# A new hand-written order for the first stage of windowed attention with two gated MLPs on one Trainium2 core

## The chip, the cores and the metric

The kernel runs on one core of a Trainium2 chip. The metric is the device time of one execution in microseconds (us); lower is better. The engines of the core are TensorE (PE, its weight loads shown apart as PEld), VectorE (DVE), ScalarE (ACT), GpSimd (POOL) and SyncE (SP), which issues all DMAs of this kernel.

## What is computed

```python
def _attn_ref(q, k, v):                      # 4 x 8 heads x 576 positions x 64
    scores = scale * np.matmul(q, k.transpose(0, 1, 3, 2))
    rel = pos[:, None] - pos[None, :]
    mask = (rel >= 0) & (rel < 64)           # each row sees itself and the 63 before it
    attn = softmax of scores under the mask
    return np.matmul(attn, v)

x = attention, as 2304 tokens x 512
x = (sigmoid(x @ w_gate) * (x @ w_val)) @ w_out        # d_ff 1536
out = ((x @ w_a) * (x @ w_b)) @ w_out2                 # d_ff 1536
```

The weights come as 64-bit floats and are decoded on the chip to pairs of a high and a low part (`wa`, `wb`, `wo` for gate, value and output). Every product is made of three: high by high, high by low, low by high.

## The kernel before

**Attention.** The 2304 tokens are 18 tiles of 128. One tile is `attention(t, dst, c0)` (line 123), a generator: each `yield` ends a step. Its steps: load `k` and `q` (three buffers for both together, tag `kq`); four transposes of `k` into a PSUM bank (`kps`), a copy of it to SBUF (`kt`, line 148, by `moved`, on VectorE or ScalarE as the table `OTHERS` says) and a copy of the 64 columns before (line 153, ScalarE or GpSimd); the same for `q` (`qps`, `qt`); 16 pairs of score products into two banks (`sps`, line 170); on VectorE four masked minima for each of the two banks (line 183, with `mask_n`, or with an edge mask from `edge_mask(s)`, line 90, for the tiles 0, 4, 9 and 13 in which a sequence starts); four exponentials for each half with their sums on ScalarE (line 189); a copy of the tile's values shifted by 64 rows (`vb`, two DMAs that wait for the load of `v`, lines 198 and 202); the denominators on VectorE (lines 207, 208) and the division on GpSimd (line 210, `pr`); transposes of `pr` (`tps`, line 218) and their copies (`pt`, line 221, `moved` again); the products with the values (`xps`, line 228); and the split of the result into `xh` (ScalarE, line 235) and `xl` (VectorE, line 237), which the first MLP reads.

**First MLP.** Turn n of `FIRST` (line 566) takes a block of 256 tokens or two and some of the 12 slices of d_ff: 12 products for the gate (`gps`) and 12 for the value (`vps`), line 428, then the hidden values on ScalarE and VectorE (`hr`, `hh`, `hl`), then their products with `wo` (`accm`, line 528). Turn 1 is block 1 with slice 0, turn 3 is block 2 with slice 0.

**What sets the order.** Up to its last element the first stage is written out by hand: the string `RAMP` (line 570) names in each letter the stream whose next step is emitted. `a` to `l` are the attention steps of tiles 0 to 11, `V` loads values, `L` loads a weight (line 354 or 352), `D` and `W` are decode steps (lines 374 to 406: ScalarE `low`, `ex`; VectorE `wi`; GpSimd `wi`, line 387; then `ex`, the high part, the low part, line 401), `K` saves a decoded weight to DRAM, `P` is a group of MLP products, `T` what follows them. `in_order()` then ties each engine to this order. So every engine has one queue, and whatever waits at its head holds all that stands behind it. SP is such a queue too: a `vb` copy that waits for its `v` holds the loads behind it.

**Banks.** The pool `ps_at` has three PSUM banks. From tile 4 on all of `kps`, `qps`, `sps`, `tps` and `xps` take them in turn, so each needs the reader of the bank three places earlier to be done. Tiles 0 to 3 transpose `k` and `q` through the two banks of `ps_acc`, and tiles 0 and 1 put their scores in the three of `ps_gv`.

The rest of the program, past the first stage, is put in order by the scheduler.

Of the kernel before, what the change touches and what calls it, by code (L numbers as in the profile page):

```python
# [10 lines left out]
F32 = mybir.dt.float32  # L11
# [4 lines left out]
ALU = mybir.AluOpType  # L16
# [5 lines left out]
def tile_window_attention_gated_mlps(ctx, tc, q, k, v, w1g, w1v, w1o, w2a, w2b, w2o, out):  # L22
    nc = tc.nc
# [14 lines left out]
    WIN = 64  # L38
    KW = P + WIN
    QSCALE = -1.0 / float(D) ** 0.5  # L40
    MASKED = 1.0e30
# [21 lines left out]
    for _ in range(7):  # L63
# [2 lines left out]


    OTHERS = {
        "k": (5, 6, 7),
        "q": (2, 4, 5, 6, 7, 8),  # L70
        "sum": (0, 7, 10),
        "p": (0, 1, 5, 8, 10),
        "norm": (10,),
        "before": (6, 7, 10, 12, 13, 14, 15, 16, 17),
    }
    mask_n = qp.tile([P, P], F32, name="mask_n")
    nc.gpsimd.memset(mask_n, 0.0)
    for e in range(2):
        rows = slice(e * WIN, (e + 1) * WIN)
        nc.gpsimd.affine_select(  # L80
            out=mask_n[rows], in_=mask_n[rows], pattern=[[1, P]], compare_op=ALU.is_ge,
# [3 lines left out]
            out=mask_n[rows], in_=mask_n[rows], pattern=[[-1, P]], compare_op=ALU.is_ge,  # L85
# [3 lines left out]

    def edge_mask(s):  # L90
        m = qp.tile([P, P], F32, tag="mask_s", name="mask_s")
        nc.vector.tensor_copy(m, mask_n)
        nc.vector.memset(m[s * WIN:(s + 1) * WIN, 0:WIN], MASKED)
        return m

    lo, hi = slice(0, D), slice(D, P)
    before, own, last = slice(0, WIN), slice(WIN, KW), slice(P, KW)
# [25 lines left out]
    def attention(t, dst, c0):  # L123
# [41 lines left out]
        for j in range(NP):  # L165
            for turn in range(2):
                for e, dims in enumerate((lo, hi)):
                    s = (e + turn) % 2
# [7 lines left out]
        for e in range(2):  # L176
            if e == 0:
                stat = small.tile([P, 3, 2, NP], F32, tag="stat", name=f"stat{t}")
                ssum, nmax, den = (stat[:, i] for i in range(3))
                mask = edge_mask(starts[0]) if starts else mask_n  # L180
            pr.append(work.tile([P, NP, P], F32, tag="pr", bufs=4, name=f"pr{t}_{e}"))
            for j in range(NP):
                nc.vector.tensor_tensor_reduce(  # L183
                    out=pr[e][:, j, :], in0=sps[e][:, j, :], in1=mask,
                    scale=1.0, scalar=LARGEST, op0=ALU.add, op1=ALU.min, accum_out=nmax[:, e, j:j + 1],
                )
            yield
            for j in range(NP):
                nc.scalar.activation(
                    out=pr[e][:, j, :], in_=pr[e][:, j, :], func=AF.Exp, bias=nmax[:, e, j:j + 1], scale=-1.0,  # L190
                    accum_out=None if t in OTHERS["sum"] else ssum[:, e, j:j + 1],
                )
            yield True
# [10 lines left out]
        for e in range(2):  # L204
            if t in OTHERS["sum"]:
                nc.vector.tensor_reduce(out=ssum[:, e], in_=pr[e], op=ALU.add, axis=AX.X)
            nc.vector.tensor_scalar(out=den[:, e], in0=ssum[:, e], scalar1=1.0e-9, scalar2=None, op0=ALU.add)
            nc.vector.reciprocal(out=den[:, e], in_=den[:, e])
            yield
            (nc.vector if t in OTHERS["norm"] else nc.gpsimd).tensor_tensor(  # L210
                out=pr[e], in0=pr[e], in1=den[:, e].unsqueeze(2).to_broadcast([P, NP, P]), op=ALU.mult
            )
            yield True
# [50 lines left out]
    def attention_units(blk):  # L264
        if blk in BACK:
            if not back:
                back.update(((i, j), quarter(i, j, "xq").bitcast(F32)) for i in range(2) for j in range(2))
        elif (0, (blk,)) not in x:
            new_x(0, group_of[blk])
        for i in range(TB):  # L270
            if blk in BACK:
                half, c0 = divmod((blk - BACK[0]) * N + i * P, W)
                yield blk, attention(blk * TB + i, [back[g, half] for g in range(2)], c0)
            else:
                yield blk, attention(blk * TB + i, x[0, (blk,)], i * P)
# [115 lines left out]
    def decode_pair(F, i, nm):  # L391
        wf, wi = wordy.pop((F, nm))
        nc.vector.scalar_tensor_tensor(  # L393
            out=wf, in0=wf, scalar=SMALLEST, in1=wi.bitcast(F32), op0=ALU.is_ge, op1=ALU.mult
        )
        yield
        pair = wts.tile([P, 2, DM], F32R, tag=f"w{nm}", name=f"w{nm}")
        wh, wl = pair[:, 0, :], pair[:, 1, :]
        nc.scalar.activation(out=wh, in_=wf, func=AF.Copy)
        yield  # L400
        nc.vector.tensor_tensor(out=wl, in0=wf, in1=wh.bitcast(F32), op=ALU.subtract)
        parts.setdefault(F, {})[nm] = (wh, wl)
        pairs[F, nm] = pair
        yield
        if nm != "o":
            nc.sync.dma_start(out=kept[F, "f"][:, i], in_=wf)
            yield
# [3 lines left out]
    def decode(F):  # L411
        for i, nm in enumerate("abo"):
            if nm not in parts.get(F, {}):
                whole(decode_words(F, i, nm))
                whole(decode_pair(F, i, nm))
                save(F, nm, pairs.pop((F, nm)))
                yield
        ready[F] = parts[F]
# [122 lines left out]
    def evacuate(phase, blk, acc, begin, end):  # L541
# [26 lines left out]


    RAMP = (  # L570
        "a6La2b2cbaDaVacb3dacbaDLbDacaca3Vb2Ddcbceb2abWdabcaedVcDfdbca2b2cdWbadgLbDbe2c2edWcWDbeVDcfbdcdbPdfe"
        "dcLd2cWfdcdc2WD2eDW2eTDfc2hdgVPgcfhLe3degdid2DVWgiLf2D2dWVe3dhfgfDfdePTfehPTefefgWegDWjT2ePfD2giWg2"
        "W2PDeWThWPefiDWTh2LTf2WTjTPf3hgD2VgLgigf2h3fDWhgTP2hgjgPTDTjWhi2jTPg2D2giDT2hgWiP2TgiDi2WPh2ViLTjTh"
        "D2TjDhgTPkWhklPkT2W2LTViWhDkjWh2TVP2WkjiDTLlLiDj2Tj2i2TWjihD2VPjTWiWjTjiTjTDLl2WPlPDjTi2TPDTjTDWkDjT"
        "PkiPWKkDTjDPj2P2W2TkTPWDPWDkDWTPDPDKP2WTDWTDTWTkTL2WD2TPLW4D2TlTPD2TWTDTDTLklWlT2KPTDKTD2PWKWT2WTKl"
        "K2D2PKlP2TLWk3lTPDWlDlWl2WkLPlDKkTlT2PWKWDWPTDW3LD2lP2T4DTDTW2PTD3lKLDTWlKlPWPDTklTP2KWTlTD2WPWTDKW"
        "K2PWKW2DkDT3DW2KPkTWT2KPkT2kTKk"
    )


# [375 lines left out]
    streams["L"] = call(lambda F=F, nm=nm: load_matrix(F, nm) for F, i, nm in order_of)  # L956
    streams["D"] = (s for F, i, nm in order_of for s in decode_words(F, i, nm))
    streams["W"] = (s for F, i, nm in order_of for s in decode_pair(F, i, nm))
    streams["K"] = call(lambda F=F, nm=nm: save(F, nm, pairs.pop((F, nm))) for F, i, nm in order_of)
    streams["P"] = call(iter(matmuls))  # L960
# [10 lines left out]
    for n, (ph, group, fcs) in enumerate(plan):  # L971
# [14 lines left out]
        for i, fc in enumerate(fcs):  # L986
            F = ph * NF + fc
# [48 lines left out]
    for n, (ph, fc) in enumerate(steps):  # L1036
# [10 lines left out]
        p = fc // PAIR  # L1047
# [35 lines left out]
        if by_seven:  # L1083
            sums = []
            for i in range(2):
                t = late["sums"].tile([P, 2, 2, CH], F32R, tag="t", name=f"s{i}")
# [83 lines left out]
```

## Time and profile before

| what | value |
|---|---|
| median of 3 runs (lowest, highest) | 950.77 us (950.51, 951.14) |
| span of the profiled execution, the one time the page gives for it | 951.4 us |
| PE busy | 935.9 us, 98% of the span |
| VectorE, ScalarE, GpSimd busy | 663.7, 470.3, 301.0 us |
| share of PE in the chain that ended last | 92% |

A row of the timeline has the start and the duration in us, the engine, the line, the operation, what it writes and reads, how many, and in brackets the idle time of the engine before it with what ended it. Matmuls overlap, so what one group of them costs is read from start to start.

### The profile page before, as it was taken

The page shows a single profiled execution, that of the slowest core. Times are in us where ns is not written, and L with a number is a line of the kernel's source. Part 1 is how long each engine was busy: PE and PEld are TensorE (multiplying, and loading weights), DVE is VectorE, ACT ScalarE, POOL GpSimd, SP SyncE. Part 2 cuts the span into 40 slices and gives each one's busy share as a digit, 9 for nine tenths or more (in the row PEclk, how much of TensorE's full clock was granted, in tenths as well). Part 3 has the DMA queues.
Part 4 walks back from the last instruction along what each step waited for, and adds up shares of the span by engine and source line. Part 5 has one row for each costly group of instructions (what it writes and reads, how often), then busy time and mean ns, then how long its engine had stood idle before and what let it go on. Part 6 is the DMA issues. An engine that isn't in the chain of part 4 may idle for free.

```text
span 951.4 us, 15582 instructions
## 1 busy us (share of the span) xinstructions
PE 935.9 (98%) x5570; PEld 785.4 (83%) x5570; DVE 663.7 (70%) x1329; ACT 470.3 (49%) x1050; POOL 301.0 (32%) x318
## 2 busy tenths in 40 slices
PE   7899999999999999999999999999999999999998
PEld 6698888888888888888888888778888888888886
DVE  6988787876776874485798455788887675464645
ACT  7887555555545565544454334554433444422321
POOL 4434232232212222222013334434431435434400
PEclk9999999999999999999999999999999999999999
DMA  8988599985575754484695445565545754442212
GB/s 210 230 223 227 195 331 316 288 264 165 168 210 170 239 192 154 136 275 165 196 366 190 155 139 171 187 208 186 188 155 184 241 203 154 155 144 91 97 45 89
DMA packets 130188, 183.20 MB, mean 193 GB/s; under 512 B 62656, under 2 KB 87488, under 8 KB 130112
## 3 DMA queue, kind: packets, MB, share of 16 engines
q1 hardware_dynamic: 130112, 182.22, 59.2%
q8 instruction: 44, 0.72, 0.3%
q14 instruction: 32, 0.26, 0.1%
HBM read 117.44 MB, written 60.29 MB: 187 GB/s over the span
## 4 chain that ended last, share of the span: by engine, by line
PE 92%; DVE 3%; DMA 2%; issue 1%; POOL 1%; ACT 1%; SPq 0%; POOLq 0%; ACTq 0%; DVEq 0%
PE gps L428 17%; PE vps L428 17%; PE qa L753 13%; PE accm L528 9%; PE acc L481 9%; PE accq L888 7%; PE qb L753 7%; PE qc L753 3%; PE accy L851 3%; PE accx L851 2%; PE xps L228 2%; PE sps L170 2%; DMA st_o<-in_moe_w_out_dram 1%; PE tps L218 1%; DVE pr L183 1%
## 5 line engine op out<-in xcount | busy, mean ns | idle before, releaser
L387 POOL TENSOR_TENSOR wi<-wi,low 128x512 int32<-128x512 int32 x72 | 104.7, 1454 | 309.8 <-DVE wi L383 263.2
L428 PE MATMUL gps<-xh,wa 128*128 128x512 f32 (+1 forms) x584 | 169.2, 356 | 0.0
L428 PE MATMUL vps<-xh,wb 128*128 128x512 f32 (+1 forms) x584 | 167.2, 353 | 0.0
L738 POOL TENSOR_TENSOR wq<-s,wq 128x256 fp32r<-128x256 f32 x96 | 76.0, 797 | 138.0 <-ACT wq L737 137.6
L428 PEld LDWEIGHTS gps<-xh,wa 128*128 128x128 f32 x584 | 104.9, 189 | 15.9 <-issue 0.3
L428 PEld LDWEIGHTS vps<-xh,wb 128*128 128x128 f32 x584 | 105.1, 189 | 15.6 <-issue 0.2
L428 PE MATMUL gps<-xl,wa 128*128 128x512 f32 (+1 forms) x292 | 103.0, 353 | 0.6 <-DVE xl L237 0.6
L428 PE MATMUL vps<-xl,wb 128*128 128x512 f32 (+1 forms) x292 | 102.7, 352 | 0.0
L528 PE MATMUL accm<-hh,wo 128*128 128x512 f32 (+1 forms) x296 | 83.5, 354 | 0.0
L753 PE MATMUL qa<-op,wq 128*128 128x512 f32 x288 | 74.3, 389 | 0.0
L772 ACT ACTIVATE r<-qa 128x512 f32<-128x512 f32 x72 | 42.7, 594 | 63.3 <-PE qa L753 60.6
L481 PE MATMUL acc<-wo,hh 128*128 128x512 f32 x240 | 73.3, 391 | 0.0
L753 PE MATMUL qb<-op,wq 128*128 128x512 f32 x288 | 73.1, 389 | 0.0
L393 DVE SCALAR_TENSOR_TENSOR ex<-ex,wi 128x512 f32<-128x512 f32 x72 | 49.8, 692 | 29.7 <-ACT ex L377 14.9
L735 POOL TENSOR_TENSOR s<-wf 128x256 f32<-128x256 f32 x48 | 38.2, 795 | 90.9 <-DMA wf<-kf 75.4
L753 PEld LDWEIGHTS qb<-op,wq 128*128 128x128 f32 x288 | 54.1, 188 | 11.2
L753 PEld LDWEIGHTS qa<-op,wq 128*128 128x128 f32 x288 | 54.0, 188 | 11.2
L439 DVE SCALAR_TENSOR_TENSOR hl<-hr,hh 128x512 fp32r<-128x512 f32 (+1 forms) x73 | 47.6, 653 | 22.2 <-ACT hh L437 21.9
L437 ACT ACTIVATE hh<-hr 128x512 fp32r<-128x512 f32 (+1 forms) x73 | 40.2, 550 | 44.5 <-DVE hr L454 27.5
L428 PEld LDWEIGHTS gps<-xl,wa 128*128 128x128 f32 x292 | 55.2, 189 | 7.7 <-DVE xl L237 0.8
L428 PEld LDWEIGHTS vps<-xl,wb 128*128 128x128 f32 x292 | 55.2, 189 | 7.6
L737 ACT ACTIVATE wq<-s 128x256 fp32r<-128x256 f32 x96 | 39.7, 414 | 39.5 <-POOL s L735 20.3
(164 smaller groups left out, 2010.4 us busy)
## 6 DMA issues: line engine op xcount, KB each, us to landing
wa<-ka SPq DMA_DIRECT2D x27, 512.0 KB, 4.3
wb<-kb SPq DMA_DIRECT2D x27, 512.0 KB, 3.5
wo<-ko SPq DMA_DIRECT2D x27, 512.0 KB, 3.8
st_o<-in_moe_w_out_dram SPq DMA_DIRECT2D x24, 512.0 KB, 4.9
kf<-ex SPq DMA_DIRECT2D x48, 256.0 KB, 4.3
ka<-wa SPq DMA_DIRECT2D x24, 512.0 KB, 3.3
kb<-wb SPq DMA_DIRECT2D x24, 512.0 KB, 4.3
ko<-wo SPq DMA_DIRECT2D x24, 512.0 KB, 3.4
```

The costliest lines, as they stand in the source:

```text
L387: nc.gpsimd.tensor_tensor(out=wi, in0=wi, in1=low, op=ALU.add)
L393: nc.vector.scalar_tensor_tensor(out=wf, in0=wf, scalar=SMALLEST, in1=wi.bitcast(F32), op0=ALU.is_ge, op1=ALU.mult)
L428: nc.tensor.matmul(ps, lhsT=a[:, c * P:(c + 1) * P], rhs=b[:, c, :], start=(n == 0), stop=(n == 3 * NP - 1))
L437: nc.scalar.activation(out=hh, in_=hr, func=AF.Copy, scale=factor)
L439: nc.vector.scalar_tensor_tensor(out=hl, in0=hr, scalar=factor, in1=hh.bitcast(F32), op0=ALU.mult, op1=ALU.subtract)
L481: nc.tensor.matmul(ps, lhsT=a[:, m * P:(m + 1) * P], rhs=b, start=begin and n == 0 and (phase == 1 or m % 2 == 0), stop=end and n == 2 and ...
L528: nc.tensor.matmul(ps[:, m], lhsT=a[:, sl], rhs=b, start=k == 0, stop=k == total - 1)
L738: nc.gpsimd.tensor_tensor(out=t[:, 1], in0=s, in1=t[:, 0].bitcast(F32), op=ALU.subtract)
L753: nc.tensor.matmul(ps, lhsT=a[:, c * P:(c + 1) * P], rhs=b[:, c, :], start=first and n == 0, stop=n == 5, skip_group_check=True,)
L772: nc.scalar.activation(out=r[n], in_=ps, func=AF.Copy)
L851: nc.tensor.matmul(bank[k], lhsT=a[n][i][:, sl], rhs=b[n][j], start=start and m == 0, stop=m == 2, skip_group_check=True,)
L888: nc.tensor.matmul(ps, lhsT=a, rhs=b, start=n == 0, stop=n == len(pairs) - 1)
```

## The change

Three things change. `RAMP` is replaced by another order of the same 645 steps. The copies that `OTHERS` names are dealt anew: on VectorE go `k` of 8 tiles (3 before), `q` of 5 (6) and `p` of 3 (5, two copies each), that is 19 copies as before; the 64 columns before are copied by ScalarE for no tile under 11 (6, 7 and 10 before), by GpSimd else. And `edge_mask` runs on GpSimd. In a tile the denominators of both halves now belong to one step. The entries `joint` and `low` are empty tuples, so what they choose is as without them.

```diff
-        "k": (5, 6, 7),
-        "q": (2, 4, 5, 6, 7, 8),
+        "k": (3, 4, 6, 7, 8, 9, 10, 11),
+        "q": (3, 4, 7, 9, 10),
         "sum": (0, 7, 10),
-        "p": (0, 1, 5, 8, 10),
+        "p": (2, 4, 10),
         "norm": (10,),
-        "before": (6, 7, 10, 12, 13, 14, 15, 16, 17),
+        "joint": (),
+        "low": (),
+        "before": (11, 12, 13, 14, 15, 16, 17),
...
-        nc.vector.tensor_copy(m, mask_n)
-        nc.vector.memset(m[s * WIN:(s + 1) * WIN, 0:WIN], MASKED)
+        nc.gpsimd.tensor_copy(m, mask_n)
+        nc.gpsimd.memset(m[s * WIN:(s + 1) * WIN, 0:WIN], MASKED)
...
-            nc.vector.tensor_scalar(out=den[:, e], in0=ssum[:, e], scalar1=1.0e-9, scalar2=None, op0=ALU.add)
-            nc.vector.reciprocal(out=den[:, e], in_=den[:, e])
+            if e == 1 or t not in OTHERS["joint"]:
+                es = slice(0 if t in OTHERS["joint"] else e, e + 1)
+                nc.vector.tensor_scalar(out=den[:, es], in0=ssum[:, es], scalar1=1.0e-9, scalar2=None, op0=ALU.add)
+                nc.vector.reciprocal(out=den[:, es], in_=den[:, es])
+        for e in range(2):
             yield
...
-        "a6La2b2cbaDaVacb3dacbaDLbDacaca3Vb2Ddcbceb2abWdabcaedVcDfdbca2b2cdWbadgLbDbe2c2edWcWDbeVDcfbdcdbPdfe"
...
+        "a2LbabcLadaca2DabDa2b3acabcbdDVeVdD2a3bca2DcWbcda2eVLDa2bWDc2d2abcabcWbebdbcbWeafcWbdbdWcefgcLWcbeDf"
...
```

SP's queue around the load of `k` for tile 5 (`k5`), with tile numbers in the names; the line numbers differ by two to seven between the files. Before:

```order
L111 DMA k4_416<-in_k_dram 64x8x64 x2
L198 DMA vb1_423<-v1_389 64x512
L202 DMA vb1_423<-v0_315 64x512
L111 DMA q4_462<-in_q_dram 64x8x64 x2
L111 DMA v2_467<-in_v_dram 128x8x64
L111 DMA k5_477<-in_k_dram 128x8x64
L111 DMA k6_527<-in_k_dram 128x8x64
L352 DMA st_o_529<-in_moe_w_out_dram 128x1024
```

And now:

```order
L113 DMA q4_428<-in_q_dram 64x8x64 x2
L113 DMA v2_431<-in_v_dram 128x8x64
L357 DMA st_o_433<-in_moe_w_out_dram 128x1024
L200 DMA vb1_509<-v1_377 64x512
L204 DMA vb1_509<-v0_372 64x512
L413 DMA kf0_142<-ex_308 128x512
L113 DMA k5_539<-in_k_dram 128x8x64
```

The output weight's load, the two `vb` copies of tile 1 and a store of 256 KB now stand ahead of `k5`.

ScalarE's queue around the exponentials of tile 1 (`pr_0`, `pr_1` with `stat_391` before and `stat_397` now). Before:

```order
L189 ACTIVATE pr_0_392,stat_391<-pr_0_392,stat_391 128x128 x4
L189 ACTIVATE pr_1_409,stat_391<-pr_1_409,stat_391 128x128 x4
L118 ACTIVATE kt_465<-kps_431 128x4x128
L374 ACTIVATE low<-st_b 128x512
L189 ACTIVATE pr_0_470,stat_469<-pr_0_470,stat_469 128x128 x4
```

And now:

```order
L191 ACTIVATE pr_0_398,stat_397<-pr_0_398,stat_397 128x128 x4
L120 ACTIVATE qt_417<-qps_407 128x512
L120 ACTIVATE pt_0_426<-tps_0_421 128x512
L120 ACTIVATE pt_1_443<-tps_1_438 128x512
L404 ACTIVATE wa<-ex 128x512
L191 ACTIVATE pr_1_445,stat_397<-pr_1_445,stat_397 128x128 x4
```

Three copies and the rounding of a weight now stand between the two halves of tile 1's exponentials.

SP's queue ahead of the shifted values of tile 5 (`vb5`). Before:

```order
L352 DMA st_o_817<-in_moe_w_out_dram 128x1024
L111 DMA v6_863<-in_v_dram 128x8x64
L198 DMA vb5_942<-v5_811 64x512
L202 DMA vb5_942<-v4_744 64x512
```

And now:

```order
L357 DMA st_o_905<-in_moe_w_out_dram 128x1024
L113 DMA q8_907<-in_q_dram 128x8x64
L113 DMA v6_915<-in_v_dram 128x8x64
L371 DMA ka0_139<-wa_450 128x1024
L413 DMA kf1_146<-ex_755 128x512
L200 DMA vb5_1004<-v5_893 64x512
L204 DMA vb5_1004<-v4_656 64x512
```

The first save of a decoded weight (`ka0`, 512 KB) and a store of 256 KB now stand ahead of `vb5`.

## Rows read from the trace of the kernel before

**Rows 1.** The page, busy share of PE in 40 slices, and PE's granted clock.
```profile
PE   7899999999999999999999999999999999999998
...
PEclk9999999999999999999999999999999999999999
```

**Rows 2.** Busy time by stretch: each engine, granted clock, DMA share, GB/s.
```profile
0.00:16.00 16.00, 11.09 (x120) 9.15 (x124) 8.94 (x50) 10.40 (x31) 6.51 (x17) 1.00 0.92 225
16.00:41.00 25.00, 20.21 (x333) 16.66 (x333) 23.26 (x103) 22.05 (x77) 12.79 (x14) 1.00 0.87 214
41.00:60.00 19.00, 17.90 (x239) 16.79 (x238) 16.44 (x61) 15.16 (x52) 7.31 (x8) 1.00 0.95 249
60.00:300.00 240.00, 240.00 (x1671) 204.84 (x1670) 183.47 (x414) 142.47 (x333) 69.37 (x55) 1.00 0.76 238
```

**Rows 3.** Timeline of PE, 11 to 41 us: landmarks on the way to turn 1.
```profile
11.48 1.10 PE L170 MATMUL sps<-kt,qt 64*64 64x128 f32 x32 [0.89 <-ACT qt L118]
...
18.35 0.65 PE L218 MATMUL tps<-ident,pr 128*128 128x128 f32 x4
...
22.05 0.34 PE L228 MATMUL xps<-pt,vb 128*64 128x64 f32 x4
...
26.77 0.63 PE L142 MATMUL kps<-ident,k 128*128 128x128 f32 x4
...
31.39 0.34 PE L228 MATMUL xps<-pt,vb 128*64 128x64 f32 x4 [1.77 <-DMA vb<-v]
```

**Rows 4.** Timeline of PE, 41 to 66 us, turn 1 to turn 3 and after.
```profile
41.06 0.36 PE L428 MATMUL gps<-xh,wa 128*128 128x256 f32 x1
...
47.00 0.34 PE L228 MATMUL xps<-pt,vb 128*64 128x64 f32 x4 [0.85 <-DMA vb<-v]
...
50.06 0.28 PE L428 MATMUL gps<-xh,wa 128*128 128x256 f32 x1
...
51.50 0.60 PE L142 MATMUL qps<-ident,q 128*128 128x128 f32 x4
51.94 0.60 PE L218 MATMUL tps<-ident,pr 128*128 128x128 f32 x4
...
57.13 0.39 PE L528 MATMUL accm<-hh,wo 128*128 128x256 f32 x1
...
58.67 0.60 PE L142 MATMUL kps<-ident,k 128*128 128x128 f32 x4
...
59.46 0.36 PE L428 MATMUL gps<-xh,wa 128*128 128x256 f32 x1
...
63.37 1.12 PE L170 MATMUL sps<-kt,qt 64*64 64x128 f32 x32
64.46 0.34 PE L228 MATMUL xps<-pt,vb 128*64 128x64 f32 x4
...
65.54 0.39 PE L528 MATMUL accm<-hh,wo 128*128 128x256 f32 x1
```

**Rows 5.** Timeline of ScalarE: price of four exponentials, of a copy, and landmarks.
```profile
17.51 0.40 ACT L189 ACTIVATE pr<-pr,stat 128x128 f32<-128x128 f32 x1 [0.18 <-DVE stat L183]
...
19.07 0.57 ACT L235 ACTIVATE xh<-xps 128x512 fp32r<-128x512 f32 x1
...
20.06 0.57 ACT L118 ACTIVATE qt<-qps 128x512 f32<-128x512 f32 x1
20.54 0.66 ACT L377 ACTIVATE ex<-st_b 128x512 f32<-128x512 f32 x1
```

**Rows 6.** Timeline of VectorE, 2 to 41 us.
```profile
2.90 0.23 DVE L92 COPY mask_s<-mask_n 128x128 f32<-128x128 f32 x1 [1.69 <-POOL mask_n L84]
...
7.59 0.29 DVE L183 CUSTOM_DVE_ANT_0 pr<-sps,mask_s 128x128 f32<-128x128 f32 x1 [4.28 <-PE sps L170]
...
29.73 0.43 DVE L380 TENSOR_SCALAR wi<-st_o 128x512 int32<-128x512 int32 x1 [1.15 <-DMA st_o<-in_moe_w_out_dram]
...
31.40 1.30 DVE L92 COPY mask_s<-mask_n 128x128 f32<-128x128 f32 x1
...
35.95 0.68 DVE L393 SCALAR_TENSOR_TENSOR ex<-ex,wi 128x512 f32<-128x512 f32 x1
36.55 0.68 DVE L116 TENSOR_SCALAR qt<-qps 128x512 f32<-128x512 f32 x1
...
40.49 0.69 DVE L237 TENSOR_TENSOR xl<-xps,xh 128x512 fp32r<-128x512 f32 x1
```

**Rows 7.** Timeline of GpSimd: a set, a copy, and an addition beside the mask's copy.
```profile
1.26 0.20 POOL L77 MEMSET mask_n<- 128x128 f32 x1
...
6.04 0.40 POOL L154 COPY kt<-kt 128x256 f32<-128x256 f32 x1 [3.17 <-ACT kt L118]
...
31.03 1.59 POOL L387 TENSOR_TENSOR wi<-wi,low 128x512 int32<-128x512 int32 x1 [2.68 <-DVE wi L383]
```

**Rows 8.** The chain that ended last, in order of time: start, us, what.
```profile
22.95 6.75 DMA st_o<-in_moe_w_out_dram
```

More of the change, by code (lines that the diff above doesn't have):

```diff
@@ L400, in decode_pair @@
         yield
-        nc.vector.tensor_tensor(out=wl, in0=wf, in1=wh.bitcast(F32), op=ALU.subtract)
+        (nc.gpsimd if 3 * F + i in OTHERS["low"] else nc.vector).tensor_tensor(
+            out=wl, in0=wf, in1=wh.bitcast(F32), op=ALU.subtract
+        )
         parts.setdefault(F, {})[nm] = (wh, wl)
@@ L570, in tile_window_attention_gated_mlps @@
     RAMP = (
-        "a6La2b2cbaDaVacb3dacbaDLbDacaca3Vb2Ddcbceb2abWdabcaedVcDfdbca2b2cdWbadgLbDbe2c2edWcWDbeVDcfbdcdbPdfe"
[L572 to L577, printed above, removed]
+        "a2LbabcLadaca2DabDa2b3acabcbdDVeVdD2a3bca2DcWbcda2eVLDa2bWDc2d2abcabcWbebdbcbWeafcWbdbdWcefgcLWcbeDf"
+        "cbcdbdeDfDcVWVeb2hgec2PdcDedcd2f2DdDeWdLiWgfhd2ecdfdDPgWfhe2fDfegd2WgTehVDeDeLigdTWVTPfgDeg2KPehW2TD"
+        "gifef2TP2WhiheLgfPfWgj2feTfWfgTfiPeTfTDfgT2DgD2fWhgPThTWDTPT2PWiVLiTDgPDgWP2hDhiThWTiPhgDigDTPhDjiLW"
+        "hkhDhTjTWjWghjPigDPTPLKLKW2DhjT2lgVWjDjT3h2TVWDWkPLjijWjKi2kPWPT2DkTih2i2jiDTj2VjhkiK2jDPiDlTlKlTji"
+        "T2PWjTijiPLjkD2jPKTjWjTDPLPW2kPD2lTlTWDlWPDTLT2PD2WDWTPkWDkDTP2LKLkTPWTDkWlWDTWDWDWk2T2W2TVDlTDTP2TD"
+        "P2TPWPDTWT2PDKlDlWTLT2l2PKklPKDWDTKl2DWDPWTDW2TDTW2LPDKTDWTDTDlPTPWkT3WTWTPWTlPlTk2lD4lPLPTkKWkTlWK"
+        "P2kKPD3W2KLlWDTD2WDTkW2TPDW2kWT2kK2TWTKT"
     )
```

## The prediction

> **What bounds the kernel now.** Read the page's slices first: PE is full in all slices but the first two and the last, and its clock is granted in full throughout [rows 1]. Then cut the front into stretches [rows 2]: PE is idle for 4.9 of the first 16 us, 4.8 of the next 25, 1.1 of the next 19, and for nothing from 60 to 300 us. So the new order can only win or lose in the first 60 us. Whatever it does there moves the end one for one, since behind it stands a queue of PE work without a gap. In the second stretch VectorE is busy for 23.3 of 25 us and ScalarE for 22.1: the front is bound by these two and by the waits between them and PE.
>
> Busy PE hides part of its waits, because the ends of matmuls are modelled. I therefore count work from start to start [rows 4]: a gate or value group of 12 products of 256 columns 1.44 us (50.06 to 51.50), four transposes 0.44 (51.50 to 51.94), the scores of a tile 1.09 (63.37 to 64.46), its value products 1.08 (64.46 to 65.54), half an output group 0.77 (57.13 to 58.67 is two).
>
> The landmark is the first product of turn 1 (it needs the last `xl` of block 1, tile 3), at 41.06 us, and then that of turn 3 at 59.46 [rows 4].
>
> **Up to turn 1.** Before, 23 groups of transposes stand ahead of turn 1, in the new list 24 (one of tile 4 came forward); scores, value products and MLP groups are as many. Equal progress would thus be 41.06 + 0.44 = 41.50. I walk the new list with the prices of the rows: a copy or rounding on ScalarE 0.48 (20.06 to 20.54), four exponentials with sums 1.56 (17.51 to 19.07) [rows 5], a full-width VectorE operation 0.60 (35.95 to 36.55) [rows 6]. Every time from here on is an estimate from these.
> - ScalarE now makes `ex` of the first weight ahead of tile 0's exponentials, so tile 1's scores start at 11.7, not 11.48 [rows 3]. SP loads `st_b` ahead of `k3` and `q2`, so `q2` lands near 14.2, and the scores of tile 2 wait for two ScalarE copies: 16.2.
> - Between tile 1's exponentials now stand three copies and a rounding, 4 x 0.5 us. The second half ends near 18.6; then denominators on VectorE and a division, and tile 1's transposes start near 21.0, not 18.35 [rows 3].
> - From here the three banks set the pace. Tile 3's scores wait for tile 0's `xl` (22.1), `kps` of tile 5 for VectorE's minima on them: 26.3 (26.77 before). Value products of tile 1: 27.2 (22.05 before); split, and the first gate group near 30.2. Value products of tile 2: 31.6 (31.39 before) [rows 3].
> - Tile 5's scores 36.1, tile 3's value products 39.1, `xh` from 40.3, `xl` from 40.9 to 41.5. Turn 1 starts at 41.5.
>
> That is the time of equal progress: the first 41 us cost the same, and this term is 0. The late values of tiles 0 and 1 cost nothing because more `k`, `q` and scores were done ahead of them; if that cover goes, the delay of 2.7 us at tile 1 appears in full.
>
> What is in this 0: the edge masks. On VectorE a copy takes 0.23 us alone, and 1.30 at 31.40, beside GpSimd's addition of 31.03 to 32.62 [rows 6, 7]. On GpSimd I bound it by the set of 128 columns and the copy of 256, 0.20 to 0.40 us [rows 7], and take 0.3: GpSimd is idle for half of that stretch [rows 2], and the copy stands ahead of tile 4's scores. The 19 copies on VectorE stay 19. The gain of some 1.4 us on VectorE at tile 4 falls into its waits for a bank and for PE, which the walk has in place of the wait of 1.15 us for `st_o` [rows 6].
>
> The Trainium skill (SBUF — State Buffer, section "Who interferes with whom") has it that VectorE and GpSimd share a pair of ports, and that whoever holds it blocks the other for the whole instruction, VectorE's operations with two SBUF inputs included. The stretched copy agrees: it ended 0.08 us after the addition. By that rule the copies on GpSimd can in turn hold VectorE: two of them in the dense stretch, up to 0.4 us each [rows 7]. As a mechanism of this kernel it would take back up to 0.8 us; the sum would then be 950.2, and I give it 0.10 of the forecast's chance below.
>
> **From turn 1 to turn 3.** Before: 18.40 us (41.06 to 59.46). Work: 4 x 1.44 + 4 x 0.77 + 2 x 1.09 + 2 x 1.08 + 8 x 0.44 = 16.70. So 1.70 us are lost, half of it in one wait for shifted values (0.85 at 47.00) [rows 4]. In the new list the same stretch has five groups of transposes, and `vb4` is issued right behind `q7`, with little outstanding. I find a single wait: `vb5` stands behind the save `ka0` and a store, 768 KB, 3.2 us at 249 GB/s [rows 2]; its issue follows `kps` of tile 8 (near 46.5), and I get 53.5 for its landing, 0.3 after PE is ready. So 0.3 in place of 1.70: **-1.40 us**. Bounds of that wait: 0, if the save overlaps the loads, and 2.0, if all 768 KB and the two loads ahead pass in sequence.
>
> **After turn 3.** PE had no idle time, and the new list has VectorE's part of turns 2 and 3 earlier. Both ends 0; work of other engines there hides behind PE's 240 us.
>
> **The sum** is a difference, 0 - 1.70 + 0.30 = -1.40 us. The profiled span of 951.4 is 0.6 above the median of the runs; I take it from the median: 950.77 - 1.40 = **949.4 us**. That is within 0.2% (1.9 us, about what a measurement of this kernel can tell from no change).
>
> **Rivals.**
> - *Faster: VectorE stays fed.* My walk lets VectorE idle for some 3.7 us before 41 us at bank waits. Its work from the first minimum (7.59) to the last `xl` of block 1 is the same 29.5 us in both lists at start-to-start prices, against 32.9 taken before (7.59 to 40.49) [rows 6]. Were it never to wait, `xl` would start at 37.1 and turn 1 at 37.7, 3.8 us under equal progress: 949.4 - 3.8 = 945.6 as the floor; half of it, 947.5, if only the hops are shorter than I price them. For it: six bank hops of the walk are each within 0.15 us of not waiting. Against: ScalarE has 1.9 us more ahead of tile 3's `xh` than before (seven copies and an exponential group more, five copies, a tanh and an edge copy fewer). It holds if turn 1 starts before 41.0.
> - *Slower: `k5` behind `st_o`.* `kps` of tile 5 is early on PE, and PE holds everything behind it. SP now issues `st_o`, two `vb` and a store ahead of `k5`; before, `k5` went ahead of `st_o`. That load took 6.75 us from issue to landing [rows 8]. Issued near 21.5, as behind `q4` in the old queue, it lands at 28.2; the other four, 0.79 MB at 225 GB/s [rows 2], at 31.7. `kps` would start 5.4 us after the 26.3 of the bank, and the banks pass this on to the end: 954.8. For it: the queue is 0.87 to 0.92 full [rows 2]. Against: all bytes up to `k5` (5.9 MB), at the rates of rows 2, are through by 26.7, and with `st_b` early the queue can fill the 0.08 it had free. It decides from 29.6 us on: then the result is above 952.7.
> - *No effect.* The order only swaps waits: where VectorE waited for `st_o`, it waits for banks, and where PE waited for `vb4`, it waits for `vb5` as long. 950.8. It lies in the forecast's band.
>
> **Chances.** Within 0.2%: 0.42 (the forecast 0.22, the port rule 0.10, no effect 0.10). Faster by more: 0.38, since every price in the walk that I rounded up shortens a chain that ends at turn 1, and 0.5 us is enough. Slower by more: 0.20. The range goes from 945.6, the floor, to 953.0; above it I leave the worse part of the `k5` case.
>
> **What would show it.** Right: turn 1 between 41.0 and 42.5 with 24 groups ahead, turn 3's first product near 57.2, no wait over 0.5 us for `vb4`, PE idle in the first 16 us a little over 4.9. The tile 1 transposes near 21 us would confirm the ScalarE step. Wrong: an idle PE ahead of `kps` of tile 5 with a DMA named (slower), a first gate group well before 30 us (faster), or any new idle slice of PE past 60 us, which nothing here expects.

## The result and the profile after

The changed kernel takes 957.88 us, median of 4 runs (957.04 to 959.36), against 950.95 us for the kernel before in the same runs. By these medians it is 0.7% slower (1.0073); the ratio on record, estimated from 4 runs of each, is 1.0067 [1.0051, 1.0083]. Run again with later experiments the change was at 1.0085 [1.0072, 1.0099]; the two intervals overlap. The profiled execution of the change took 958.25 us with a span of 956.2. In all executions whose time and span are listed, the time is 1.7 to 2.2 above the span; the profiled execution of before, with a span of 951.4, must therefore have taken some 2.4 us more than its median. That is why the two spans differ by 4.8 us and the medians by 6.9.

The page of the changed kernel, PE's busy share and its granted clock:

```profile
PE   6799999999999999999999999999999999999998
...
PEclk9999999999999999999999999999999999999999
```

The stretches of the changed kernel (length, then busy time of PE, PE's weight loads, VectorE, ScalarE, GpSimd, granted clock, DMA share, GB/s), to be read against [rows 2]:

```profile
0.00:16.00 16.00, 10.88 (x110) 8.95 (x110) 7.83 (x36) 9.81 (x23) 6.99 (x19) 1.00 0.88 213
16.00:41.00 25.00, 18.23 (x292) 14.54 (x293) 22.39 (x93) 21.54 (x79) 13.01 (x14) 1.00 0.89 231
41.00:60.00 19.00, 18.58 (x268) 17.18 (x268) 16.90 (x63) 15.12 (x52) 9.75 (x11) 1.00 0.94 255
60.00:300.00 240.00, 237.97 (x1639) 202.31 (x1638) 185.55 (x419) 140.55 (x331) 69.56 (x58) 1.00 0.73 231
```

PE's idle time grew from 4.8 to 6.8 us in the second stretch, fell from 1.1 to 0.4 in the third, and there is 2.0 us of it past 60 us, where before there was none. The landmarks in the timeline of PE, in the order of [rows 3, 4] (tile 0's and tile 1's scores, tile 1's transposes, `kps` of tile 5, tile 1's value products, the first gate group, turn 1, turn 3):

```profile
7.12 1.10 PE L172 MATMUL sps<-kt,qt 64*64 64x128 f32 x32 [0.69 <-ACT qt L120]
...
12.28 1.10 PE L172 MATMUL sps<-kt,qt 64*64 64x128 f32 x32 [1.08 <-ACT qt L120]
...
22.84 0.66 PE L223 MATMUL tps<-ident,pr 128*128 128x128 f32 x4 [0.58 <-POOL pr L215]
...
28.76 0.63 PE L144 MATMUL kps<-ident,k 128*128 128x128 f32 x4 [2.13 <-ACT pr L191]
...
29.75 0.34 PE L233 MATMUL xps<-pt,vb 128*64 128x64 f32 x4
...
33.12 0.36 PE L435 MATMUL gps<-xh,wa 128*128 128x256 f32 x1
...
45.10 0.36 PE L435 MATMUL gps<-xh,wa 128*128 128x256 f32 x1
...
60.83 0.28 PE L435 MATMUL gps<-xh,wa 128*128 128x256 f32 x1
```

Turn 1 starts at 45.10 where equal progress is 41.50: 3.6 us late. `kps` of tile 5 waits for its load, though the row names ScalarE's exponentials: `k5` was issued at 22.72 us, landed at 28.62, and `kps` starts 0.14 behind it. In `w3_again` and `u12_masks_den` (below) the profile names the load itself at this place. In `v3_both`, where the load is early, the same `kps` starts at 26.45, beside ScalarE's exponentials of tile 3, so it does not need them.

Turn 3 follows after 15.73 us, against 18.40 before: the lag is down to 2.2. Further on the two lists reach the same state. A late landmark, the last scores ahead of 305 us (tile 14), stands at 296.95 us before and at 302.42 now: 5.5 late, so another 3.3 us are lost behind turn 3. The waits of PE in the changed kernel, 60 to 300 us (us in total, times, longest), show 2.0 of them. For the other 1.3 no wait of PE is in the profile; where they go stays open. The three waits:

```profile
PE accm L535 <- ACT gacc L511: 0.8, 1, 0.8
PE accm L535 <- DVE hl L446: 0.6, 1, 0.6
PE vps L435 <- ACT hr L455: 0.6, 1, 0.6
```

They stand at 128, 153 and 148 us. Ahead of the first, ScalarE waited twice for a store of a decoded half weight, `kf`, which must be out before its buffer `ex` is written again (timeline of ScalarE):

```profile
113.33 0.67 ACT L382 ACTIVATE ex<-st_a 128x512 f32<-128x512 f32 x1 [3.42 <-DMA kf<-ex]
...
125.86 0.66 ACT L382 ACTIVATE ex<-st_o 128x512 f32<-128x512 f32 x1 [2.17 <-DMA kf<-ex]
```

So there are three questions: which part of the change costs, what holds the first 45 us, and what is lost past 60. Steps are named by what they make: `k5` is tile 5's load of `k`, `st_o` the load of the first third weight, `den1` tile 1's denominators.

### The profile page after: what moved, and what is told of

It is laid out like the page before. It is cut to its first block, busy times and chain, and to the rows that moved or that the text cites. A ratio compares the mean times of both kernels' runs of the same rounds, so it can differ in the third digit from the quotient of the medians.

```text
span 956.2 us, 15573 instructions
## 1 busy us (share of the span) xinstructions
PE 937.3 (98%) x5570; PEld 785.3 (82%) x5570; DVE 668.8 (70%) x1321; ACT 469.9 (49%) x1048; POOL 306.1 (32%) x328
## 4 chain that ended last, share of the span: by engine, by line
PE 89%; DVE 4%; DMA 3%; issue 1%; ACT 1%; SPq 1%; POOL 1%; ACTq 0%; DVEq 0%; POOLq 0%
PE gps L435 16%; PE vps L435 15%; PE qa L760 13%; PE acc L488 9%; PE accm L535 8%; PE accq L895 7%; PE qb L760 7%; PE qc L760 3%; PE accy L858 3%; PE accx L858 2%; PE xps L233 2%; PE tps L223 1%; PE sps L172 1%; DMA k<-in_k_dram 1%; PE kps L144 1%
## 5 line engine op out<-in xcount | busy, mean ns | idle before, releaser
L398 DVE SCALAR_TENSOR_TENSOR ex<-ex,wi 128x512 f32<-128x512 f32 x72 | 52.2, 725 | 25.3 <-POOL wi L392 13.1
L535 PEld LDWEIGHTS accm<-hh,wo 128*128 128x128 f32 x296 | 52.6, 189 | 8.4 <-ACT gacc L511 1.2
```

What stands on the lines that cost most here:

```text
L398: nc.vector.scalar_tensor_tensor(out=wf, in0=wf, scalar=SMALLEST, in1=wi.bitcast(F32), op0=ALU.is_ge, op1=ALU.mult)
L535: nc.tensor.matmul(ps[:, m], lhsT=a[:, sl], rhs=b, start=k == 0, stop=k == total - 1)
```

## Experiments

All ratios are against the kernel before on the same chip, in 4 to 6 runs of the kernel (12 of `v4_before_st_o`) and 9 to 17 of before (the first ratio of the table: 4 and 4).

| kernel | ratio | 95% interval |
|---|---|---|
| the change; again (`w3_again`) | 1.0067; 1.0085 | 1.0051 to 1.0083; 1.0072 to 1.0099 |
| `e1_old_list`: all but the list | 1.0067 | 1.0054 to 1.0080 |
| `e2_new_list_only`: only the list | 1.0158 | 1.0143 to 1.0173 |
| `x2_deal`: only the deal of copies | 1.0084 | 1.0068 to 1.0099 |
| `x1_masks_den`: only masks and denominators | 1.0046 | 1.0033 to 1.0059 |
| `u12_masks_den`: all but masks and denominators | 1.0059 | 1.0039 to 1.0079 |
| `e3_new_head`, `e4_new_tail` | 1.0064, 1.0085 | 1.0050 to 1.0079, 1.0070 to 1.0100 |
| `u3_early_store`, `u4_k5`, `u5_add` | 1.0073, 1.0063, 1.0071 | each +/- 0.0021 |
| `v1_k5_first`, `v2_tail16`, `v3_both` | 1.0078, 1.0056, 1.0048 | each +/- 0.0013 |
| `v4_before_st_o` | 1.0007 | 0.9994 to 1.0020 |
| `w1_add_both`, `w2_den_first`, `w4_tail9` | 1.0054, 1.0050, 1.0050 | each +/- 0.0014 |

### The parts of the change alone

`e1_old_list` is the changed kernel with the list of before, `e2_new_list_only` the reverse:

```diff
     RAMP = (
-        "a2LbabcLadaca2DabDa2b3acabcbdDVeVdD2a3bca2DcWbcda2eVLDa2bWDc2d2abcabcWbebdbcbWeafcWbdbdWcefgcLWcbeDf"
...
+        "a6La2b2cbaDaVacb3dacbaDLbDacaca3Vb2Ddcbceb2abWdabcaedVcDfdbca2b2cdWbadgLbDbe2c2edWcWDbeVDcfbdcdbPdfe"
...
```

> The changed kernel with the old list of 645 steps: the new deal of copies, the edge masks on GpSimd and the denominators in one step stay. Theory A (the order of the steps costs the 6.9 us): the time is that of before, 951.0, within 1 us. Theory B (the deal and the masks cost it: ScalarE and VectorE get their work at the wrong place): above 955. Rival C (both cost about half): 953.5 to 955.

> The kernel before with nothing changed but the list of 645 steps; copies, masks and denominators are the old ones. Theory A (the order costs it): 957 to 958.5, as the whole change. Theory B (deal and masks cost it): 951, within 1 us. A time above 959 would say that the new deal belongs to the new list and wins something back in it.

`e1_old_list`, at 958.7 us, lies where theory B has it. `e2_new_list_only`, at 967.3, is above what either theory has, as the third reading said it would be: the new deal belongs to the new list. The list alone costs 15 us, all the rest alone 6.3, both together 6.9, so the two costs do not add. The way to read this is that list and deal are one plan. A list says when each engine gets a step; put the copy on another engine and it stands in that engine's order at a place chosen for other work. In `e2_new_list_only`, the second stretch:

```profile
16.00:41.00 25.00, 18.43 (x248) 14.39 (x248) 19.38 (x87) 15.37 (x60) 11.21 (x12) 0.86 0.76 195
```

ScalarE is busy for 15.4 of 25 us, against 21.5 in the change. There it waits 4.8 us for PE's value products and 2.4 for VectorE, and VectorE 3.3 for ScalarE. PE's clock, 0.86 on average, is lower there too. Two later runs split the rest. `x2_deal` is the kernel before with the new table:

```diff
-        "k": (5, 6, 7),
-        "q": (2, 4, 5, 6, 7, 8),
+        "k": (3, 4, 6, 7, 8, 9, 10, 11),
+        "q": (3, 4, 7, 9, 10),
...
-        "p": (0, 1, 5, 8, 10),
+        "p": (2, 4, 10),
...
-        "before": (6, 7, 10, 12, 13, 14, 15, 16, 17),
+        "before": (11, 12, 13, 14, 15, 16, 17),
```

> The kernel before with the new deal of copies and nothing else. The changed kernel with the old list, which has the deal, the masks and the denominators, was at 1.0067. Theory N (the deal makes all of that): 1.0065 +/- 0.0015, with the scores of tile 2 or 3 waiting over 1 us for ScalarE's copy of q. Rival (masks and denominators have a share): 1.004 or less.

`x1_masks_den` has the other two parts, with the old list and deal:

```diff
-        nc.vector.tensor_copy(m, mask_n)
+        nc.gpsimd.tensor_copy(m, mask_n)
...
         for e in range(2):
             if t in OTHERS["sum"]:
                 nc.vector.tensor_reduce(out=ssum[:, e], in_=pr[e], op=ALU.add, axis=AX.X)
             nc.vector.tensor_scalar(out=den[:, e], in0=ssum[:, e], scalar1=1.0e-9, scalar2=None, op0=ALU.add)
             nc.vector.reciprocal(out=den[:, e], in_=den[:, e])
+        for e in range(2):
             yield
```

> The kernel before with the edge masks copied by GpSimd and both halves' denominators in one step; list and deal are the old ones. With them undone the changed kernel was at 1.0059 against 1.0067 to 1.0085. Theory N (they cost nothing): ratio 1.000 +/- 0.001. Rival (the denominators in one step hold VectorE at the front, which has no slack): ratio 1.002 or more.

The deal alone costs 1.0084, more than expected (1.0065 +/- 0.0015); PE waits 4.1 us in four places for ScalarE's `qt`, as expected. Masks and denominators cost 1.0046, where 1.000 was expected: the rival had 1.002 or more. The timeline of VectorE in `x1_masks_den`:

```profile
16.75 0.92 DVE L209 TENSOR_SCALAR stat<-stat 128x4 f32<-128x4 f32 x1 [0.29 <-ACT pr L189]
...
27.04 0.17 DVE L209 TENSOR_SCALAR stat<-stat 128x4 f32<-128x4 f32 x1 [1.52 <-ACT pr L189]
```

These are the denominators of tiles 1 and 2. Before, a step of its own stood there for the first half, which needs only that half's exponentials. In one step for both halves it also waits for the second half's, and the minima of the next tile stand behind it on VectorE. The first of the two rows also shows 0.92 us for what took 0.17 elsewhere, beside GpSimd's division (16.60 to 17.64 us). So the 4.2 us come at least in part from the joined step; how they divide between its wait, the division beside it and the masks was not tested, since no run has one part alone. In this execution PE later waited 1.77 us for `pt`, ahead of 19.18 us, and ran at the lower clock around it; its five executions list a mean clock of 0.996 to 0.998, those of before 0.998 to 1.0 (same columns as above):

```profile
18.60:25.30 6.70, 6.12 (x60) 5.67 (x64) 4.85 (x22) 4.34 (x13) 1.16 (x2) 0.50 0.62 150
```

Under the new list the denominators come later, and undoing both parts makes no difference clear of noise:

> The changed kernel with two of its parts undone: the edge masks are copied by VectorE again, and each half's denominators are a step of its own again; list and deal are the new ones. Theory (these two parts cost nothing; it is list and deal that do): the time of the changed kernel, 1.007 of before, within 0.1%. Rival (the two halves' denominators in one step hold VectorE ahead of tile 1's minima, 14.70 against 12.79 us): tile 1's minima start over 0.5 us earlier and the ratio is 1.005 or less.

The ratio is 1.0059 against 1.0067 and 1.0085, each with an interval of 0.0013 to 0.0020 to either side. Tile 1's minima do start 1.4 us earlier (13.30 in place of 14.70, the rival's sign), but turn 1 comes at 45.6: `k5` landed at 29.0 there, PE waits 2.19 us for it, and the gain ends in that wait.

### Front and rest

`e3_new_head` takes 210 steps of the new list and then the old order of what is left, `e4_new_tail` 209 of the old list and then the new order; both are otherwise the changed kernel.

> The changed kernel with the new list up to its fifth group of products (210 steps, some 50 us), and behind it the steps that are left in their old order. In the changed kernel's trace turn 3 starts 2.2 us later than equal progress allows, and some 3.3 us more are lost between 60 and 200 us. Theory H (loss of the front and loss behind it are separate, and the order behind the cut makes the second): 953 +/- 0.8, and no idle PE between 100 and 160 us. Rival (the second loss is a late effect of the front, a backlog of ScalarE and VectorE): 957 to 958 as the whole change.

> The changed kernel with the old list up to the same point (209 steps), and behind it the steps that are left in their new order. Theory H: the front is as before and the later loss of 3.3 us stays: 954.3 +/- 0.8, with ScalarE waiting for a store of kf for over 2 us near 110 and 124 us. Rival (all is made in the front): 951, within 1 us.

`e3_new_head` took 958.1 us, as its rival has it; `e4_new_tail` took 960.7, above both readings. The expectations were too simple: the old list is no undisturbed base once the deal is new (`e1_old_list`). What they give is two differences. With the old front the new order behind it costs 1.0085 - 1.0067, 1.7 us, with intervals that overlap; with the new front it is 1.0067 or 1.0085 against 1.0064. The second is no clean price either: in the profiled execution of `e3_new_head` PE's clock was at 0.50 in three stretches of the front, and turn 1 came at 47.2. In `e4_new_tail` ScalarE waits 13.9 us for `kf` stores between 60 and 230 us, in `e3_new_head` 1.4: the waits belong to the new order behind the cut.

### The first 45 us

`u4_k5` moves `k5` to right behind `st_o`, and ScalarE's first step on `st_o` behind tile 3's exponentials; `u5_add` moves GpSimd's first addition behind tile 0's divisions:

```diff
  L_o0
+ k5
...
- k5
...
- low_o0
  kps5 norm12 pt11 tps02 exp03
+ low_o0
```

```diff
- add_a0 low_b0
  vb0 den0 norm00 min01 before2 norm10
+ add_a0 qps2 exp01 low_b0
```

> The changed kernel with k5's load moved to right behind the load of st_o, ahead of two loads of shifted values and a store, and ScalarE's first step on st_o moved behind a copy and four exponentials of tiles 1 and 3, which now wait 1.8 us for that load. Theory K (the front is late because k5 is): k5 lands near 27.5 in place of 28.6, its transposes start at 27.9 in place of 28.8, turn 1 follows 1 to 2 us earlier than 45.1, and the time falls by about as much: ratio 1.0055 +/- 0.0010. Rival (ScalarE and VectorE are behind anyway, the banks pass it on): turn 1 at 45 and ratio 1.007.

> The changed kernel with GpSimd's first addition of a weight moved behind its two divisions of tile 0 (and the steps that need it behind tile 1's first exponentials). In the changed kernel a denominator operation of VectorE takes 1.28 us beside that addition (0.17 elsewhere), and tile 1's minima start at 14.70 us. Theory P (that hold sets the front back): the minima start near 13.3, tile 1's transposes near 21.5 in place of 22.8, and turn 1 comes 1 us earlier, ratio 1.006. Rival (k5, which lands at 28.6, sets kps of tile 5 and all behind it): tile 1 is earlier, kps of tile 5 is not, and the ratio stays at 1.007.

Both went the way of their rivals: turn 1 at 45.2 and 45.0, ratios unchanged within their intervals. In `u4_k5` `k5` was issued at 21.08 us and still took 7.6 to land, with the 512 KB of `st_o` ahead of it; the 5.9 us of the change from 22.72 end at the same 28.6. In `u5_add` the addition's hold was gone (below), but `kps` of tile 5 stood at 28.6. So `v1_k5_first` takes the bytes away: `k5` and two `vb` ahead of `st_o`. `v4_before_st_o` does the opposite in the kernel before.

```diff
  q4 v2
- L_o0
+ k5
...
  vb1
+ L_o0
...
- low_o0
  kps5 norm12 pt11 tps02 exp03 xps1 min13 qt4
+ low_o0
```

> The changed kernel with the load of st_o put behind k5 and the two shifted values of tile 1 (SP: q4, v2, k5, two vb, st_o, store kf), and ScalarE's first two steps on st_o behind its copy for tile 4. In every execution profiled so far kps of tile 5 starts 0.10 to 0.15 us after k5 has landed (28.8 after 28.6 in the changed kernel, 26.8 after 26.6 before), whether its load was issued at 21.1 or at 23.3 us. Theory K (the bytes ahead of k5 set the front): without 768 KB ahead of it k5 lands by 26, its transposes start by 26.5, turn 1 starts 1.5 to 2.5 us earlier than 45.1, the ratio falls from 1.007 to 1.005. Rival (ScalarE and VectorE are as late): the transposes wait for a bank until 28 or later, turn 1 stays at 45, ratio 1.007.

> The kernel before with one step moved: the load of st_o goes ahead of those of k5 and k6, as in the new list. Theory K (the bytes ahead of k5 set the front): k5 lands some 2.2 us later than 26.6, kps of tile 5 starts near 28.9 in place of 26.8, turn 1 comes 1 to 2 us later than 41.1, ratio 1.0015 +/- 0.0010. Rival (the front has slack there): kps of tile 5 is late, turn 1 is not, ratio 1.000.

`v1_k5_first` by itself decided little: `k5` landed at 24.0, but PE had the lower clock in two stretches of the profiled execution, and turn 1 stayed at 45.1. `w4_tail9` (below) has the same front, the lower clock in two stretches as well, and turn 1 at 45.3. The same front in `v3_both`, with the clock at 1.00 in the front, is the clean reading (timeline of PE: `kps` of tile 5, transposes of tile 2, value products of tile 1, the first gate group, turn 1):

```profile
26.45 0.63 PE L144 MATMUL kps<-ident,k 128*128 128x128 f32 x4
...
28.01 0.63 PE L223 MATMUL tps<-ident,pr 128*128 128x128 f32 x4 [0.93 <-POOL pr L215]
28.57 0.34 PE L233 MATMUL xps<-pt,vb 128*64 128x64 f32 x4
...
32.02 0.36 PE L435 MATMUL gps<-xh,wa 128*128 128x256 f32 x1
...
43.98 0.36 PE L435 MATMUL gps<-xh,wa 128*128 128x256 f32 x1
```

`kps` of tile 5 comes 2.3 us earlier and waits for no load; tile 2's transposes then wait for GpSimd's division, and 1.1 us are left at turn 1. That is what `k5`'s place was worth in this pair of executions, which start alike (tile 0's scores at 7.12 in both) and have the clock at 1.00 in both. The times do not resolve it: `v1_k5_first` is at 1.0078, and `v3_both` and `v2_tail16`, which differ in the front alone, overlap.

The next limit also shows here. From 24.95 to 31.10 us VectorE is busy for 6.05 of 6.15 us, and GpSimd's two divisions for tile 2, from 26.32 on, take 2.59. In all five profiled executions with `k5` early (`v1`, `v3`, `w1`, `w2`, `w4`) those transposes wait 0.92 to 0.96 us for the division. Turn 1 follows 16.0 us behind their start in each, whatever the clock did ahead of them; from `kps` of tile 5 it is 17.5 us, and 15.2 in the prediction's walk.

In the kernel before the same bytes ahead of `k5` set its transposes back by 1.1 us (27.9, behind a wait of 0.61 us for the load), yet turn 1 came at 40.3, earlier than before. VectorE's wait of 1.15 us for `st_o` is gone there, which may be the reason, and the ratio is 1.0007: there the place of `k5` had slack. The other end shows in the changed kernel run again:

> The changed kernel, unedited, on the chip of the runs beside it: 1.0067 +/- 0.001 of before. Its landmarks (tile 0's scores, kps of tile 5, turn 1) tell how far they vary from execution to execution: tile 0's scores, whose work ahead is the same in both kernels, start between 6.3 and 7.1 us in the executions so far, so kps of tile 5 is expected between 27.5 and 28.8 and turn 1 between 44.4 and 45.2.

The timeline of PE, at `kps` of tile 5:

```profile
30.70 0.63 PE L144 MATMUL kps<-ident,k 128*128 128x128 f32 x4 [3.21 <-DMA k<-in_k_dram]
```

Two stretches of the same execution, columns as above:

```profile
27.50:30.70 3.20, 0.00 (x0) 0.03 (x1) 3.17 (x12) 2.76 (x11) 2.87 (x4) 1.00 1.01 203
31.50:34.50 3.00, 3.00 (x37) 2.23 (x35) 0.50 (x1) 0.98 (x2) 0.75 (x1) 0.50 0.97 251
```

The same program, and `k5` took 7.63 us and landed at 30.6. PE stood idle for 3.2 us, then worked at a clock of 0.50, and turn 1 came at 48.2, outside the expected 44.4 to 45.2. The ratio, expected at 1.0067 +/- 0.001, was 1.0085.

Two more edits tried what is left of the front, both on `v3_both`: the addition again, and tile 1's `vb`, denominators and divisions ahead of tile 2's second minima.

```diff
  exp11
+ vb1 den1 norm01 norm11
  exp02 xh0
- vb1
  L_o0 min12 wl_a0
- den1
  kps4
- norm01
  qt3
```

> The kernel with k5 first and the old order past 316 steps, and GpSimd's first addition behind its two divisions of tile 0 as well. With k5 landed by 24.6 us its transposes start at 26.4, the transposes of tile 2 at 28.0, turn 1 at 44.0 us. Theory P (tile 1's minima, held from 13.3 to 14.7 beside that addition, are what is late next): turn 1 near 43, ratio 1.004 against 1.005. Rival (VectorE does the same work later, in idle time that appears behind it): turn 1 at 44.0 +/- 0.3, same ratio.

> The same kernel (k5 first, old order past 316 steps) with tile 1's shifted values, denominators and divisions ahead of tile 2's second minima and of a subtraction of the first weight. Theory D (the new list holds tile 1 back: its transposes start at 22.8 us, at 18.4 before, and its value products at 28.6, at 22.1 before): they start near 21.5, and turn 1 comes by 43 in place of 44.0; ratio 1.004. Rival (tile 1's late values are covered by scores done ahead, as the prediction had it): turn 1 at 44.0 +/- 0.3.

Neither theory P nor theory D held. In `w2_den_first` turn 1 is at 43.8, against 44.0, as its rival has it; in `w1_add_both` it is at 44.6, later than both theory and rival. In `w1_add_both` the hold is gone (timeline of VectorE, tile 0's first denominators),

```profile
11.86 0.17 DVE L211 TENSOR_SCALAR stat<-stat 128x4 f32<-128x4 f32 x1
```

where the changed kernel has 1.28 us beside GpSimd's addition and set:

```profile
11.87 1.28 DVE L211 TENSOR_SCALAR stat<-stat 128x4 f32<-128x4 f32 x1
```

and turn 1 gained nothing by it. In `w2_den_first` tile 1's transposes start at 21.9 in place of 22.8, and turn 1 is 0.2 us earlier, in an execution that had the lower clock between 12 and 15.4 us.

### Past 60 us

`u3_early_store` issues each `kf` store in the step that computes it:

```diff
             out=wf, in0=wf, scalar=SMALLEST, in1=wi.bitcast(F32), op0=ALU.is_ge, op1=ALU.mult
         )
+        if nm != "o":
+            nc.sync.dma_start(out=kept[F, "f"][:, i], in_=wf)
         yield
```

> The changed kernel with each store of a decoded half weight (kf) issued in the step that computes it, two steps earlier in SP's queue. In the changed kernel ScalarE waits 10.4 us for such stores between 60 and 230 us, 3.4 and 2.2 of it at 113 and 126 us, and PE is idle for 0.8, 0.6 and 0.6 us at 128, 148 and 152 us. Theory S (these idle spells come from the late stores): the waits of ScalarE fall below 4 us, PE has no idle time past 100 us, and the time falls by 1.5 to 2.5 us, to a ratio of 1.0050 +/- 0.0010. Rival (VectorE and GpSimd's additions hold the hidden values up whatever the stores do): the same idle time of PE, ratio 1.007.

PE gained nothing, against theory S. ScalarE's waits for stores went from 10.4 to 1.2 us, a wait of 7.9 us for a load of `st_o` behind them on SP came in their place, and PE waits as it did:

```profile
PE accm L536 <- DVE gacc L514: 0.7, 1, 0.7
PE accm L536 <- DVE hl L447: 0.6, 1, 0.6
PE vps L436 <- ACT hr L456: 0.6, 1, 0.6
```

`v2_tail16` keeps the new list for 316 steps (16 groups of products, about 110 us) and goes on in the old order; `v3_both` has the front of `v1_k5_first` as well; `w4_tail9` cuts that at step 260, about 60 us.

> The changed kernel with its own list for 316 steps (16 groups of products, some 110 us), and behind it the steps that are left in their old order. The kernel with early stores took away ScalarE's wait for stores and PE stayed idle as long at 128, 148 and 152 us, so the stores are not the cause. Theory T (the order of the steps behind 110 us is): PE is not idle past 110 us and the ratio falls by 0.002, from 1.007 to 1.005. Rival (a backlog carried over from the first 110 us): idle spells of PE of the same sum come in other places.

> Both edits of the two runs beside it in one kernel. If the front's loss (k5) and the later loss (order past 110 us) are separate, the two gains add: ratio 1.003 +/- 0.001. If a gain in the front is only lost later, it is that of the better of the two.

> The kernel with k5 first, and the old order already from step 260 on (9 groups of products, about 60 us). With the cut at 316 steps PE's idle time past 110 us is gone, but 1.8 us of new idle time stands between 75 and 100 us, at the cut. If the order past the cut is what costs, all idle time past 60 us falls below 0.7 us and the ratio is 1.003; if each cut makes its own loss (VectorE and ScalarE are some us behind PE from the front on), it is 1.005 again.

In `v2_tail16` PE has no idle time past 100 us, and the late landmark (302.42 in the change) stands at 301.54; at turn 1 and turn 3 the two are within 0.1 us (`v2_tail16` started 0.8 us earlier and lost that again while the clock was low from 28 to 31 us). In `v3_both` it is at 300.21, 2.2 earlier, of which 1.1 came from the front: in the traces the gains add. Its ratio of 1.0048 is the lowest of those with the new front, but above the expected 1.003 +/- 0.001, and within the noise of `v2_tail16`, `w2_den_first` and `w4_tail9`. The waits of PE in `v3_both`, 60 to 300 us, show a new loss between 75 and 100 us, ahead of the cut at about 110:

```profile
PE xps L233 <- DVE kt L118: 0.9, 1, 0.9
PE tps L223 <- DVE qt L118: 0.9, 1, 0.9
```

With the cut at 260 it is 1.5 us, and the ratio the same. So 2 us of idle time go with the order past 110 us, and 0.9 us net by the landmark, which the ratios do not resolve; whether an order exists that loses nothing behind this front was not tried. No version beat the kernel before.

## Why the prediction was wrong

The forecast was 949.4 with a range up to 953.0; the result is 957.9. One reading under the sum was wrong: it set the span of the profiled execution, 951.4, against the median time, 950.77, and found 0.6 between them. A span is about 2 us shorter than its time, so that execution was some 2.4 us slower than the median, and the waits that the sum takes from it (1.70 us between turn 1 and turn 3) are those of an execution slower than that median. By its steps:

- **Up to turn 1: "this term is 0", measured +3.6.** This is the first step that failed. Walk against trace: tile 1's scores 11.7 / 12.28, its transposes 21.0 / 22.84, `kps` of tile 5 26.3 / 28.76, first gate group 30.2 / 33.12, turn 1 41.5 / 45.10. The error grows at every hop. 1.1 us of it is `k5`, which the walk let start at its bank's time and not at its landing; that size comes from one pair of traces, `v3_both` against the change.

  The other 2.5 us arise behind `kps` of tile 5. With `k5` early that step is only 0.15 behind the walk, tile 1's value products are 1.4 behind, the first gate group 1.8, turn 1 2.5. The walk gave 0.9 us to the first of these hops, with no wait in it; the trace has 2.1, 0.93 of them PE's wait for GpSimd's division of tile 2, while VectorE has no free time. Which engine would have to be faster there was not tested: only GpSimd's first hold and tile 1's delay were moved, and they gained nothing, or 0.2 us.

  Tile 0's scores stood at 7.12 in place of 6.43 with the same instructions ahead: the first transposes took 1.06 us, before 0.60 to 0.74, for a reason that no row shows. Executions of the other kernels have 6.3 to 7.1, with the same steps, so this is chance; what it is worth at turn 1 is not shown.
- **The rival of `k5`** had the mechanism and the wrong size. The main walk set it aside because "all bytes up to `k5`" would be through by 26.7; it landed at 28.6, and at 30.6 in another execution, past the 29.6 us from which the rival was to decide. Its price of 5.4 us was too high: 1.1 at 28.6, and about 3 more at 30.6 with the lower clock.
- **The cover for tile 1's late values** held as far as it was tried: tile 1 0.9 us earlier gave 0.2 at turn 1, and no ratio clearly better.
- **From turn 1 to turn 3: -1.40 us, right in size.** Some 15.7 to 15.8 follow from the sum, which takes 0.3 for a wait for `vb5` on 15.4 of work; 15.73 was measured, with no wait for `vb4` or `vb5`. The wait for `vb4` fell away as forecast; the 0.3 came out by luck, since the wait that was to give it is not there.
- **After turn 3: "both ends 0", measured +3.3.** This is the second step that failed, and its sign was named: "any new idle slice of PE past 60 us". The reason given was PE's 240 us without idle time before the change. That showed that the old order had cover, and not how much the new one leaves. At 128 to 153 us ScalarE and VectorE were just late: 2.0 us of idle PE, of which the old order past 110 us takes all away, at the price of 1.5 to 1.8 elsewhere. The other 1.3 us stay open.
- **Masks and denominators.** The masks had a price near nothing and the denominators no term at all. Under the new list no difference clear of noise came of them, so this step was not wrong here. But it rested on no reason for the denominators: under the old list the two parts cost 4.2 us, and VectorE's new wait for the second half's exponentials is in that trace. The prediction did not ask what the joined step newly waits for.
- **The port rule** fits the first hold in the trace: a denominator operation took 1.28 us, 0.17 without GpSimd beside it. Taking that one hold away gained nothing at turn 1. Later VectorE operations beside GpSimd stay stretched, as in the `v3_both` trace (0.82 us for a `wi` of `st_o` that takes 0.42 elsewhere); what these cost was not tested.
- **Chances.** "Slower" had 0.20 on one mechanism with one threshold. The sum had a walk with over ten hops of an engine each, and no term for hops that are longer than the durations in the rows.

## What to carry to other kernels

A hand-made order and the table that deals its steps to engines are one object: changing either alone cost 15 and 7 us here, both together 7. An idle-free PE says that the present order hides the other engines' work, and not how near they are to being late; to predict a new order, ask for each waiting instruction how early its operand was. And when two steps are joined, price the wait that the first half now inherits from the second.

## What the runs showed of the hardware

The clock of TensorE fell within the front. In the changed kernel run again, PE was idle from 27.5 to 30.7 us and then had 0.50, the 1.2 GHz level, from 31.5 to 34.5; in `x1_masks_den` from 18.6 to 25.3. The Trainium skill (TensorE: Matmul & The Clock Gate, Part 1) has it that the hardware sets this clock by how busy the engine has lately been, and `w3_again` agrees. The idle time just ahead does not settle it, though: the first execution of the change kept 1.00 behind 2.13 us of idle PE at 28.76, and `v2_tail16` had 0.53 from 28 to 31 us behind 1.39. In `w3_again` `kps` of tile 5 was 1.9 us later than in the first profile and turn 1 3.1, so the wait was followed by a further loss of 1.2.

Such stretches are frequent here: 12 of the 20 profiled executions have one at about 0.50 within the first 48 us, among them five of the kernels that are compared by turn 1 above (`v1_k5_first`, `v2_tail16`, `w2_den_first`, `w4_tail9`, `u5_add`). With the same list up to there, `v1_k5_first` has turn 1 at 45.06, with such stretches, and `v3_both` at 43.98, without: a turn 1 from a single execution can be off by 1 us.

A load's landing varied more than expected in one program: `k5` took 5.9 us in one execution and 7.6 in the other, issued at 22.7 and 22.9, with a DMA share of 1.01 and 1.03 in between. Turn 1, which waits for it, came at 45.1 and 48.2. Whether this makes the whole time spread is not shown: the ratios of the two sets of runs, 1.0067 and 1.0085, have intervals that overlap.
